# The low part of v's last 64 tokens moves from VectorE to GpSimd, the first exponentials wait for an early dummy one, and the order table is new

## The chip, the cores and the metric

The kernel runs on one core of one Trainium2 chip. Its time is the device time of an execution in microseconds (us). Three timed runs of the kernel before gave 339.54, 340.26 and 340.89 us; their median, 340.26 us, is the time that the changed kernel's is held against. A profile was taken in another execution, which took 337.29 us.

## The reference

Two blocks follow each other. The first is causal attention, for 4 batches and 12 heads, 448 tokens and a head size of 64, in float32:

```python
scores = scale * np.matmul(q, k.transpose(0, 1, 3, 2))
scores = np.where(mask, -1000000000.0, scores)
scores = scores - np.max(scores, axis=-1, keepdims=True)
attn = np.exp(scores)
attn = attn / (np.sum(attn, axis=-1, keepdims=True) + 1e-09)
return np.matmul(attn, v)
```

Its output, with the heads side by side, is the x (4 x 448 x 768) of a gated MLP, in which tokens are mixed through w_sg (448 x 448):

```python
h = x @ w_in                                  # 768 -> 1024, then the tanh form of gelu
u, v = (h[..., :d_ff // 2], h[..., d_ff // 2:])
v_n = (v - mu) / np.sqrt(var + 1e-06) * g_ln  # mean and variance over the 512 columns
v_s = np.einsum('ts,bsd->btd', w_sg, v_n) + b_sg[None, :, None]
return (x + (u * v_s) @ w_out)
```

## The kernel before

**Attention.** Two heads are one pair; there are 24 pairs, six to a batch. `pair(p)` loads q and k of a pair (`qk`), multiplies them on TensorE in two groups (`score(0)` and `score(1)`, line 431, tile `s` in PSUM), adds the mask and takes the negated row maxima on VectorE (line 446, `ngm`), and takes the exponentials on ScalarE (line 454), which sum their rows into `sm` and write the tile `P`. VectorE inverts the sums (lines 464 to 466), and two DMAs spread the result over the partitions (`rd`, then `rb`). For pairs 0 to 7 (below `FLIP`) TensorE transposes `P` (line 496, tiles `tx` and `ty`) and ScalarE or VectorE copies the result to `B` (lines 503 and 501). For the others VectorE transposes 32 x 32 blocks (line 484) and DMAs place them. TensorE then multiplies `B` by v (line 522, tile `o`), VectorE scales the result by `rb` into `xt` (line 549), and `keep_x` splits it into a rounded high part and the rest (lines 555 to 560, tile `x`). `P` has three buffers of two heads each, named P_90, P_91 and P_92 in the program's order; pair 2 of batch 0 uses P_92, pair 3 uses P_90 again.

**Weights.** All matrix multiplications of the MLP take float32 as a high part and a low part, three products for one. `split_w64` makes these parts of `w_in` and `w_out`: one operation on ScalarE (line 366), two on VectorE (368 and 370) and two on GpSimd (373 and 374), for each of 12 pieces of `w_in` (tile `vn`) and 16 of `w_out` (tile `g`).

**MLP of a batch.** `mlp(b)` has four parts: v for 128 tokens at a time and a last one of 64 tokens (`m` = 64), u, the mixing by `wsg` (tile `m<-wsg,vn`) and the output product (`m<-g,wout`); all multiplications are issued at line 577. v is normalised: statistics on VectorE, the power on GpSimd (line 621), the scaling on ScalarE (line 626). Then ScalarE copies it into a rounded high part, and the rest is subtracted: for the blocks of 128 tokens by GpSimd (line 631), for the last 64 tokens by VectorE (line 636). The tile `vn3` of these 64 tokens has the high part in partitions 0 to 63 and the low part in partitions 64 to 127, so that one multiplication takes both. Every mixing group ends with two multiplications by `vn3`.

**The order.** Nothing is issued while the functions run. `Order.add` records each operation with its engine and what it depends on, and gives it the next number. `run` then issues all operations in the order of the table `ORDER`, a list of these numbers written out by hand. `plan` only asserts that what an operation depends on stands ahead of it. Each engine works off its own operations in that order, and the framework adds the semaphores; SyncE issues all DMAs. The durations, sizes and `port` flags that `add` is given are read by nothing that runs. Seven small multiplications on a zeroed tile (`warm`, numbers 4 and 5 to 11, line 339) and one exponential of a constant column (number 3, line 330) do no work for the result.

Of the kernel before, what the change touches and what calls it, by code (L numbers as in the profile page):

```python
# [12 lines left out]
AF = mybir.ActivationFunctionType  # L13
ALU = mybir.AluOpType
# [211 lines left out]
def attention_gated_mlp(ctx: ExitStack, tc: tile.TileContext, qk, vP, w_in, g_ln, w_sgT, b_sg, w_out, out):  # L226
    nc = tc.nc
# [4 lines left out]
    DH = DF // 2  # L232
# [533 lines left out]
```

## Time and profile before

| what | value |
|---|---|
| median of three timed runs | 340.26 us (339.54 to 340.89) |
| the profiled execution | 337.29 us, of which the span of the instructions 335.5 us |
| TensorE (PE), matmuls | 324.1 us busy, 97% of the span, 2590 records |
| VectorE (DVE) | 251.0 us, 75% |
| ScalarE (ACT) | 208.5 us, 62% |
| GpSimd (POOL) | 175.9 us, 52% |
| chain that ended last | PE 93%, ACT 4%, DMA 1%, DVE 1% |
| mean granted TensorE clock | 0.994 of full speed |

The span begins with the first instruction and ends with the last. The profiled execution has 1.79 us outside it. "Busy" is the time in which at least one instruction of the engine ran. The share is over the whole span, so it says little of a single stage: ScalarE's 62% is a mean over a stage in which it never rests and one in which it mostly waits. The chain that ended last is followed back from the last instruction, at each step to what released it or to the instruction before it on its engine. In the rows below, PEld is TensorE's loading of weights, which overlaps its multiplications.

### The profile page before, as it was taken

What the parts mean: (1) busy time and instruction counts of PE and PEld (TensorE: products, weight loads), DVE (VectorE), ACT (ScalarE), POOL (GpSimd) and SP (SyncE); (2) the same over time, 40 slices, a digit from 0 to 9 for tenths busy, and PEclk for the clock granted to TensorE, in tenths of its full rate; (3) what the DMA queues carried; (4) which work ended last, traced back from release to release, by engine and by line L of the source; (5) the groups of instructions that cost most, each with busy time, mean ns of one, the idle gap of its engine ahead of it and who ended that gap; (6) DMA issues with size and microseconds to landing.
All of it is one profiled execution on the core that took longest, in us unless ns stands there. A gap on an engine that the chain in (4) does not pass through costs nothing.

```text
span 335.5 us, 7568 instructions
## 1 busy us (share of the span) xinstructions
PE 324.1 (97%) x2590; PEld 266.3 (79%) x2591; DVE 251.0 (75%) x762; ACT 208.5 (62%) x674; POOL 175.9 (52%) x225
## 2 busy tenths in 40 slices
PE   5699999999999999999999999999999999999995
PEld 3467678768887987878888978878989987889994
DVE  4899898999999888967977597889788531644613
ACT  1999999999894637666784526486674302355210
POOL 4258766888986964020535942014256824132691
PEclk9899999999999999999999999999999999999999
DMA  7889968595583688638747858739437440010004
GB/s 227 312 247 307 277 218 267 177 288 160 130 265 103 178 215 235 197 98 226 217 127 214 229 150 204 195 95 243 101 104 206 91 159 3 0 55 2 18 36 164
DMA packets 30965, 56.55 MB, mean 169 GB/s; under 512 B 6096, under 2 KB 15056, under 8 KB 30928
## 3 DMA queue, kind: packets, MB, share of 16 engines
q1 hardware_dynamic: 30928, 56.08, 57.5%
q8 instruction: 20, 0.33, 0.4%
q14 instruction: 17, 0.14, 0.1%
HBM read 33.39 MB, written 5.90 MB: 117 GB/s over the span
## 4 chain that ended last, share of the span: by engine, by line
PE 93%; ACT 4%; DMA 1%; DVE 1%; issue 0%; ACTq 0%; DVEq 0%
PE m L577 65%; PE o L522 13%; PE s L431 11%; ACT P L454 3%; PE ty L496 2%; PE tx L496 2%; DMA qk<-in_qk_dram 1%; PE m L339 0%; ACT L454 0%; ACT vn L366 0%; ACT B L503 0%; DVE s L446 0%; DVE res L702 0%; DVE ngm L446 0%; ACTq L454 0%
## 5 line engine op out<-in xcount | busy, mean ns | idle before, releaser
L454 ACT ACTIVATE P<-s,ngm 128x320 f32<-128x320 f32 (+3 forms) x240 | 102.7, 460 | 28.1 <-DVE ngm L446 19.7
L446 DVE CUSTOM_DVE_ANT_0 s<-s,mask 64x64 f32<-64x64 f32 (+3 forms) x192 | 77.6, 435 | 7.5 <-PE s L431 5.8
L577 PE MATMUL m<-win,x 128*128 128x512 f32 (+1 forms) x264 | 65.9, 399 | 0.0
L577 PE MATMUL m<-g,wout 128*128 128x448 f32 x288 | 61.1, 367 | 0.0
L577 PE MATMUL m<-x,win 128*128 128x448 f32 x288 | 61.1, 367 | 0.0
L577 PEld LDWEIGHTS m<-x,win 128*128 128x128 f32 x288 | 53.9, 188 | 5.0
L577 PEld LDWEIGHTS m<-g,wout 128*128 128x128 f32 x288 | 53.9, 188 | 5.0
L577 PEld LDWEIGHTS m<-win,x 128*128 128x128 f32 (+1 forms) x264 | 47.4, 183 | 11.7
L454 ACT ACTIVATION_READ_ACCUMULATOR P<-s,ngm 128x1 f32 (+1 forms) x240 | 55.1, 233 | 0.0
L431 PE MATMUL s<-qk 64*64 64x64 f32 (+5 forms) x768 | 45.2, 371 | 5.0 <-DMA qk<-in_qk_dram 4.4
L431 PEld LDWEIGHTS s<-qk 64*64 64x64 f32 x768 | 30.7, 139 | 21.6 <-issue 8.5
L522 PE MATMUL o<-B,vraw 128*64 128x64 f32 (+4 forms) x672 | 45.0, 291 | 0.0
L522 PEld LDWEIGHTS o<-B,vraw 128*64 128x64 f32 x672 | 32.8, 137 | 12.7 <-issue 4.5
L484 DVE STREAM_TRANSPOSE P<-P 128x1024 f32<-128x1024 f32 x32 | 38.2, 1224 | 0.7 <-DMA B<-P 0.6
L577 PE MATMUL m<-wsg,vn 128*128 128x448 f32 x176 | 38.3, 369 | 0.0
L621 POOL TENSOR_TENSOR mv<-mv,mhalf 128x1 f32<-128x1 f32 (+1 forms) x16 | 10.0, 626 | 49.0 <-DVE mv L619 40.7
L577 PEld LDWEIGHTS m<-wsg,vn 128*128 128x128 f32 x176 | 32.6, 188 | 3.6 <-DVE vn L636 0.4
L558 POOL TENSOR_TENSOR x<-xt,x 128x448 fp32r<-128x448 f32 x24 | 27.5, 1148 | 14.5 <-ACT x L557 14.2
L702 DVE TENSOR_TENSOR res<-m,res 128x448 f32<-128x448 f32 (+1 forms) x25 | 14.8, 603 | 23.2 <-PE m L577 15.2
L586 DVE SCALAR_TENSOR_TENSOR tmp<-tmp,m 128x448 f32<-128x448 f32 (+1 forms) x28 | 17.9, 640 | 16.2 <-ACT tmp L585 16.0
L673 POOL TENSOR_TENSOR tmp<-tmp,g 128x448 f32<-128x448 f32 x16 | 18.3, 1152 | 18.8 <-DVE tmp L669 18.8
L585 ACT ACTIVATE tmp<-m 128x448 f32<-128x448 f32 (+1 forms) x28 | 15.5, 562 | 20.3 <-PE m L577 19.2
(76 smaller groups left out, 410.8 us busy)
## 6 DMA issues: line engine op xcount, KB each, us to landing
B<-P SPq DMA_DIRECT2D x64, 256.0 KB
qk<-in_qk_dram SPq DMA_DIRECT2D x24, 448.0 KB
vn<-in_w_in_dram SPq DMA_DIRECT2D x12, 512.0 KB
vraw<-in_vP_dram SPq DMA_DIRECT2D x24, 256.0 KB
rb<-rd SPq DMA_DIRECT2D x24, 224.0 KB
out_dram<-res SPq DMA_DIRECT2D x9, 448.0 KB
g<-in_w_out_dram SPq DMA_DIRECT2D x16, 192.0 KB
out_dram<-res SPq DMA_DIRECT2D x5, 224.0 KB
```

Source lines behind the costliest of these rows:

```text
L431: nc.tensor.matmul(out=s[z][bk].t[64 * h:64 * h + 64, col:col + n], lhsT=qk_.t[r, 0, q0:q0 + 64], rhs=qk_.t[r, 1, k0:k0 + n], start=True, ...
L446: nc.vector.tensor_tensor_reduce(out=o, in0=i, in1=mk, scale=-0.125, scalar=3e38, op0=ALU.add, op1=ALU.min, accum_out=ngm[ib[z]][c][0:m])
L454: act(n, lambda c=c, m=m, k0=k0, n=n, bk=bk, col=col, off=off, kc=kc, i=i, z=z: nc.scalar.activation(out=P[i][0:m, off:off + n], in_=s[z][ ...
L484: dve(PW, lambda z=z: nc.vector.transpose(A[ia][:, :, :, z, :].rearrange("p g t k -> p t g k"), P[ib[z]]), Pk[z] + [kp], Ak, 1.105)
L496: nc.tensor.transpose(out, P[ib[z]][:, col:col + 128], ident)
L522: nc.tensor.matmul(out=dst(o.t[r]), lhsT=vr.t[:, c, r], rhs=src(z), start=first and n == 0, stop=last and n == len(lst) - 1)
L558: pool_tt(S, lambda: nc.gpsimd.tensor_tensor(out=y.t[:, S + 64:], in0=x.t, in1=f(y.t)[:, 0:S], op=ALU.subtract), [x, y], [(y, 1)])
L577: nc.tensor.matmul(out=ps.t[0:l().shape[1], 0:n], lhsT=l(), rhs=rr(), start=(k == 0), stop=(k == len(mms) - 1))
L585: act(n, lambda: nc.scalar.activation(out=z(), in_=h(), func=AF.Square), [ps], [t])
L586: dve(n, lambda: nc.vector.scalar_tensor_tensor(out=z(), in0=z(), scalar=1.0 / GC, in1=h(), op0=ALU.add, op1=ALU.mult), [ps], [t])
L673: pool_tt(S, lambda z=z, u=u: nc.gpsimd.tensor_tensor(out=z(), in0=z(), in1=u.t, op=ALU.mult), [u], [t])
L702: dve(hi - lo, lambda rr=rr, ps=ps, z=z, lo=lo, hi=hi: nc.vector.tensor_tensor(out=rr.t[:, z, lo:hi], in0=ps.t[:, lo:hi], in1=rr.t[:, z, l ...
```

## The change

- The low part of v's last 64 tokens is no longer one subtraction on VectorE, from partitions 0 to 63 into 64 to 127. ScalarE writes two more copies, the rounded one and the exact one, into partitions 64 to 127, and GpSimd subtracts there.
- Every exponential of the attention names "table", which the dummy exponential (number 3) writes, as something it depends on.
- `ORDER` is a new table. It has 1891 numbers, not 1883 (one VectorE operation less, two ScalarE and one GpSimd operations more in each of four batches), so the numbers behind the first such place are shifted.
- Some durations, sizes and `port` flags in `add` differ. `run` reads none of them.

```diff
 ORDER = (
-    84, 85, 86, 1, 4, 0, 2, 89, 87, 90, 96, 88, 95, 98, 91, 92, 97, 99, 93, 94, 125, 126, 128, 127, 12, 18, 13, 103,
+    0, 4, 1, 3, 2, 84, 125, 5, 6, 7, 8, 9, 166, 85, 86, 89, 87, 90, 96, 88, 95, 98, 97, 91, 93, 92, 99, 94, 100, 103,
...
-                    [s[z][bk], ("ngm", i, c), kp, ks] + ([("P", i, k - 1)] if k == 1 else [("P", i, 2)] if k == 4 else []),
+                    [s[z][bk], ("ngm", i, c), kp, ks, "table"] + ([("P", i, k - 1)] if k == 1 else [("P", i, 2)] if k == 4 else []),
...
                 y = buf(one, "vn3", [128, DH], F32R)
                 act(DH, lambda y=y, z=z: nc.scalar.activation(out=y.t[0:64], in_=z(), func=AF.Copy), [t], [y], True)
-                dve(DH, lambda y=y, z=z: nc.vector.tensor_tensor(out=y.t[64:128], in0=z(), in1=f(y.t)[0:64],
-                                                                 op=ALU.subtract), [t, y], [(y, 1)])
+                act(DH, lambda y=y, z=z: nc.scalar.activation(out=y.t[64:128], in_=z(), func=AF.Copy), [t], [(y, 1)], True)
+                act(DH, lambda t=t, z=z: nc.scalar.activation(out=t.t[64:128], in_=z(), func=AF.Copy), [], [t], True)
+                pool_tt(DH, lambda y=y, t=t: nc.gpsimd.tensor_tensor(out=y.t[64:128], in0=t.t[64:128],
+                                                                     in1=f(y.t)[64:128], op=ALU.subtract), [t], [(y, 1)])
```

Three lines are added in all, so a line behind line 64 of the kernel has a number higher by 1, and behind line 636 by 3.

**How the order moves, ScalarE in the first pairs.** Before, these rows stand ahead of the last exponential of pair 2 (tile P_92). L366 is the first step of a split of `w_in`; P_90 here is pair 3.

```order
L503 ACTIVATE B<-tx 128x512
L454 ACTIVATE P_92,sm_119<-s,ngm_111 128x320
L366 ACTIVATE vn<-vn 128x512
L454 ACTIVATE P_92,sm_119<-s,ngm_114 128x128
L454 ACTIVATE P_92,sm_119<-s,ngm_110 128x128
L366 ACTIVATE vn<-vn 128x512
L454 ACTIVATE P_92,sm_119<-s,ngm_115 128x320
L454 ACTIVATE P_92,sm_119<-s,ngm_112 128x448
L454 ACTIVATE P_92,sm_119<-s,ngm_110 64x64
L454 ACTIVATE P_92,sm_119<-s,ngm_109 64x64
L454 ACTIVATE P_90,sm_117<-s,ngm_96 128x448
L454 ACTIVATE P_92,sm_119<-s,ngm_114 64x64
```

In the changed kernel these rows stand ahead of the same place.

```order
L504 ACTIVATE B<-tx 128x512
L455 ACTIVATE P_92,sm_119<-s,ngm_116 128x448
L504 ACTIVATE B<-tx 128x512
L455 ACTIVATE P_92,sm_119<-s,ngm_113 64x64
L455 ACTIVATE P_92,sm_119<-s,ngm_112 128x448
L455 ACTIVATE P_92,sm_119<-s,ngm_111 128x320
L455 ACTIVATE P_92,sm_119<-s,ngm_109 64x64
L455 ACTIVATE P_92,sm_119<-s,ngm_110 128x128
L455 ACTIVATE P_92,sm_119<-s,ngm_110 64x64
L455 ACTIVATE P_92,sm_119<-s,ngm_115 128x320
L455 ACTIVATE P_92,sm_119<-s,ngm_114 128x128
L455 ACTIVATE P_92,sm_119<-s,ngm_114 64x64
```

From the start to this place ScalarE has five of the splits' operations and one exponential of pair 3 before, and three and none in the changed kernel; the 30 exponentials of pairs 0 to 2 and the six copies to `B` are the same. Up to the last exponential of pair 3 it is five splits and seven copies to `B` before, three and six in the changed kernel. The load of the exponential's table and the dummy exponential are ScalarE's first two instructions in the changed kernel; before, the load stands directly ahead of the first exponential of pair 0.

On SyncE, the loads of q and k of pairs 0, 1 and 2 are the first three in the changed kernel; before, pair 2's is the sixth, behind two pieces of `w_in` and one of v. Ahead of the first small DMA of the sums (`rd`) stand 13 loads in the changed kernel and 12 before.

**TensorE ahead of the first transposes of pair 2.** Before, these rows stand there; `o` is the product by v of pairs 0 and 1, `ty` the transposes, and the `s` rows are the first group of scores of pair 4.

```order
L522 MATMUL o<-B,vraw 64x448 x2
L522 MATMUL o<-B,vraw 64x320 x2
L522 MATMUL o<-B,vraw 64x64 x2
L522 MATMUL o<-B,vraw 64x128 x2
L522 MATMUL o<-B,vraw 64x64 x4
L496 MATMUL ty<-ident,P_92 128x128 x8
L431 MATMUL s<-qk 64x448 x2
L431 MATMUL s<-qk 64x384 x2
L431 MATMUL s<-qk 64x64 x2
```

In the changed kernel:

```order
L432 MATMUL s<-qk 64x448 x2
L432 MATMUL s<-qk 64x384 x2
L432 MATMUL s<-qk 64x64 x2
L523 MATMUL o<-B,vraw 64x64 x2
L523 MATMUL o<-B,vraw 64x128 x2
L523 MATMUL o<-B,vraw 64x64 x2
L523 MATMUL o<-B,vraw 64x448 x2
L523 MATMUL o<-B,vraw 64x320 x2
L523 MATMUL o<-B,vraw 64x64 x2
L523 MATMUL o<-B,vraw 64x128 x2
L523 MATMUL o<-B,vraw 64x64 x2
L497 MATMUL ty<-ident,P_92 128x128 x8
```

The first group of scores of pair 4 has moved from behind these transposes to ahead of them. Everything else that stands ahead of them is the same in both: the scores of pairs 0 to 3, the transposes and products by v of pairs 0 and 1, and the seven multiplications on zeros. Of these seven all stand ahead of pair 3's scores before; in the changed kernel five are TensorE's first work and two stand behind the first transposes of pair 0.

**The last 64 tokens of batch 1.** Before, VectorE subtracts (`vn_2449` is the `vn3` of batch 1) between operations of u:

```order
L466 STREAM_TRANSPOSE rT_122<-rs 128x32
L590 SCALAR_TENSOR_TENSOR g<-tmp,m 128x448
L484 STREAM_TRANSPOSE P_92<-P_90 128x8x4x32 x2
L586 SCALAR_TENSOR_TENSOR tmp<-tmp,m 128x448
L636 TENSOR_TENSOR vn_2449<-tmp,vn_2449 64x512
L586 SCALAR_TENSOR_TENSOR tmp<-tmp,m 128x448
```

In the changed kernel GpSimd does (`vn_2383` is the same tile); `x<-xt,x` are the low parts of a later pair's x, `res` the sums for batch 0's output.

```order
L561 TENSOR_TENSOR x<-xt,x 128x64
L692 TENSOR_TENSOR res<-x 128x448
L559 TENSOR_TENSOR x<-xt,x 128x448
L692 TENSOR_TENSOR res<-x 128x448
L639 TENSOR_TENSOR vn_2383<-tmp,vn_2383 64x512
L559 TENSOR_TENSOR x<-xt,x 128x448
```

The subtraction has moved to another engine's queue, behind a low part of x. On TensorE, the number of MLP multiplications between the end of v's last 64 tokens and the first mixing multiplication by `vn3` goes from 88 to 100 in batch 0, 88 to 79 in batch 1, 82 to 85 in batch 2, and stays 70 in batch 3.

## Rows read from the trace of the kernel before

**Rows 1.** Stages, TensorE: start:end, length, busy (records), granted clock, DMA share, GB/s.

```profile
8.83:22.65 13.82, 9.97 (x74) 0.88 0.81 279
22.65:60.00 37.35, 37.35 (x403) 1.00 0.86 268
140.00:331.87 191.87, 191.83 (x1375) 1.00 0.47 129
331.87:335.50 3.63, 0.00 (x0) 0.93 0.27 101
```

**Rows 2.** Stages, ScalarE, columns as above; the clock is still TensorE's.

```profile
7.07:31.09 24.02, 24.00 (x94) 0.93 0.86 286
31.09:50.00 18.91, 18.91 (x72) 1.00 0.83 258
84.00:100.00 16.00, 13.62 (x43) 1.00 0.72 203
```

**Rows 3.** The chain that ended last: start us, us, what.

```profile
3.92 1.88 PE s L431 x8
...
21.40 1.24 PE m L339 x5
...
28.04 1.02 PE ty L496 x8
29.07 0.92 PE s L431 x8
...
252.80 19.90 PE m L577 x96
```

**Rows 4.** Timeline, ScalarE: start us, us, operation; in brackets the idle time before.

```profile
7.07 1.28 ACT L454 ACT_TABLE_LOAD   x1 [7.07 <-DVE ngm L446]
8.37 0.63 ACT L454 ACTIVATE P<-s,ngm 128x448 f32<-128x448 f32 x1
...
23.70 0.81 ACT L366 ACTIVATE vn<-vn 128x512 f32<-128x512 f32 x1
24.26 0.65 ACT L454 ACTIVATE P<-s,ngm 128x320 f32<-128x320 f32 x1
...
29.41 0.75 ACT L503 ACTIVATE B<-ty 128x512 f32<-128x512 f32 x1
29.88 0.53 ACT L454 ACTIVATE P<-s,ngm 128x128 f32<-128x128 f32 x1
...
30.52 0.48 ACT L454 ACTIVATE P<-s,ngm 64x64 f32<-64x64 f32 x1
```

**Rows 5.** Two stretches, TensorE, columns as in rows 1.

```profile
7.30:14.12 6.82, 3.73 (x48) 1.00 1.02 389
14.13:17.53 3.40, 3.17 (x26) 0.50 0.46 132
```

**Rows 6.** Line 636: durations ns min/median/max; then who waited for it.

```profile
L636 DVE TENSOR_TENSOR vn<-tmp,vn x4: 685/685/2120, 97.8 to 308.4; 64x512 fp32r<-64x512 f32 x4
...
PEld m L577: 0.4, 2
```

**Rows 7.** Timeline: VectorE and TensorE in batch 1, GpSimd and VectorE in batch 2.

```profile
173.67 0.69 DVE L636 TENSOR_TENSOR vn<-tmp,vn 64x512 fp32r<-64x512 f32 x1
...
174.75 4.64 PE L577 MATMUL m<-wsg,vn 128*128 128x448 f32 x22
...
242.66 3.38 POOL L689 TENSOR_TENSOR res<-x 128x448 f32<-128x448 f32 x3
...
244.48 2.12 DVE L636 TENSOR_TENSOR vn<-tmp,vn 64x512 fp32r<-64x512 f32 x1 [1.02 <-ACT vn L635]
```

**Rows 8.** Groups by line: count, then busy us, mean ns, idle before us.

```profile
L631 POOL TENSOR_TENSOR vn<-tmp,vn 128x512 fp32r<-128x512 f32 x12 | 15.9, 1331 | 18.5 <-ACT vn L630 18.4
...
L635 ACT ACTIVATE vn<-tmp 64x512 fp32r<-64x512 f32 x4 | 2.5, 630 | 0.1
```

**Rows 9.** Waits: who for whom, us in total, times, longest us.

```profile
POOL x L558 <- ACT x L557: 14.2, 3, 6.6
```

More of the change, by code (lines that the diff above doesn't have):

```diff
@@ L328, in attention_gated_mlp @@
     od.add("pool", 2.4, consts3, w=["P", "sm", ("wsg", "pad")])
-    od.add("act", 0.2, lambda: nc.scalar.activation(out=pad[:, 0:1], in_=mhalf, func=AF.Exp), ["sm0"], ["table"])
+    od.add("act", 1.35, lambda: nc.scalar.activation(out=pad[:, 0:1], in_=mhalf, func=AF.Exp), ["sm0"], ["table"])
     def warm():
@@ L467, in inv @@
                                 rs.unsqueeze(2).broadcast_to([128, 2, 4, 4]))
-        od.add("dve", 0.42, inv, sk + [ks], [("rT", ip)])
+        od.add("dve", 0.573, inv, sk + [ks], [("rT", ip)])
         rb = buf(some[SLOTS["rb"]], "rb", [128, S])
@@ L474, in pair @@
         dma(lambda: nc.sync.dma_start(out=rb.t, in_=bass.AP(
-            tensor=rd[ip].tensor, offset=rd[ip].offset, ap=[[512, 8], [0, 16], [1, S]])), [("rd", ip)], [rb], 320e3, dur=0.56)
+            tensor=rd[ip].tensor, offset=rd[ip].offset, ap=[[512, 8], [0, 16], [1, S]])), [("rd", ip)], [rb], 360e3, dur=0.56)
         Pk = [[("P", i, c) for c in range(5)] for i in ib]
@@ L579, in group, with gelu2 @@
             pe(per * len(mms[a:a + cut]), go, rd, [ps])
-    def gelu2(ps, m, n, dst=None):
+    def gelu2(ps, m, n, dst=None, port=False):
         t = buf(three, "tmp", [128, 512])
@@ L586, in gelu2 @@
         dve(n, lambda: nc.vector.scalar_tensor_tensor(out=z(), in0=z(), scalar=1.0 / GC, in1=h(), op0=ALU.add,
-                                                      op1=ALU.mult), [ps], [t])
+                                                      op1=ALU.mult), [ps], [t], port=port)
         act(n, lambda: nc.scalar.activation(out=z(), in_=z(), func=AF.Tanh, scale=GS * GC), [], [t], True)
@@ L590, in gelu2 @@
         dve(n, lambda: nc.vector.scalar_tensor_tensor(out=z() if dst is None else d.t, in0=z(), scalar=1.0, in1=h(),
-                                                      op0=ALU.add, op1=ALU.mult), [ps, t], [d])
+                                                      op0=ALU.add, op1=ALU.mult), [ps, t], [d], port=port)
         return t, z
@@ L614, in mlp @@
                                                                      op=ALU.add), [ps], [hs])
-                t, z = gelu2(hs, m, DH)
+                t, z = gelu2(hs, m, DH, port=True)
             st, mv = buf(two, "st", [128, 6]), buf(two, "mv", [128, 3])
@@ L622, in mlp @@
                 out=mv.t[0:m, 1:2], in0=mv.t[0:m, 1:2], in1=mhalf[0:m], op=ALU.pow), ["sm0"], [mv])
-            od.add("dve", 0.07, lambda mv=mv, m=m: nc.vector.tensor_scalar(
+            od.add("dve", 0.125, lambda mv=mv, m=m: nc.vector.tensor_scalar(
                 out=mv.t[0:m, 2:3], in0=mv.t[0:m, 0:1], scalar1=mv.t[0:m, 1:2], scalar2=-1.0, op0=ALU.mult, op1=ALU.mult),
@@ L626, in mlp @@
             act(DH, lambda mv=mv, z=z, m=m: nc.scalar.activation(
-                out=z(), in_=z(), func=AF.Identity, scale=mv.t[0:m, 1:2], bias=mv.t[0:m, 2:3]), [mv], [t], True)
+                out=z(), in_=z(), func=AF.Identity, scale=mv.t[0:m, 1:2], bias=mv.t[0:m, 2:3]), [mv], [t], True, 2)
             if m == 128:
```

179 rows, old and new, of the table ORDER are left out of this document.

## The prediction

> **What bounds the kernel now.** I read the stages of TensorE first. From 22.65 us on it is busy for 37.35 of 37.35 us, then up to 331.87 us for 191.83 of 191.87 us in the last long stretch [rows 1]. The last 3.63 us hold no multiplication. The change leaves TensorE's useful work as it is, so the end can move by two things only: how much of this work is done before TensorE saturates at 22.65 us, and new waits behind it. In the stretch before, TensorE is busy for 9.97 of 13.82 us [rows 1], and part of that does nothing for the result: five of the seven multiplications on zeros take 1.24 us of the chain [rows 3], and the clock is at 0.50 (1.2 of 2.4 GHz) for 3.40 us [rows 5].
>
> Next I ask what TensorE waits for in that head. ScalarE starts at 7.07 us with the load of a table [rows 4] and is busy for 24.00 of 24.02 us and then for 18.91 of 18.91 us, to 50 us [rows 2]. So ScalarE, which gives the exponentials, is the tight engine of the head, and TensorE's lead can hardly grow by more than ScalarE's.
>
> **The change, part by part.**
>
> *Table load.* Before, ScalarE loads the table after VectorE's first maxima, at 7.07 us, and the first exponential begins at 8.37 us [rows 4]: 1.30 us on ScalarE's path. Now load and dummy exponential stand first in its queue, where it idles for 7.07 us. The dummy waits for one small VectorE operation behind the zeroing of the multiplications' tile, all of it ahead of the first load of q and k, so this cover is wide. Gain: 1.30 us.
>
> The Trainium skill (ScalarE: Activation LUTs, What ACT_TABLE_LOAD costs) adds a drain to each switch and comes to about 2.66 us in all; by that rule the term would be 1.36 us larger and the sum with it. The trace does not agree: the exponential begins 0.02 us behind the load [rows 4].
>
> *ScalarE's new order.* Up to the last exponential of pair 3 (30.52 us), two splits of w_in and one copy to B have gone from ahead of it to behind it. A split takes 24.26 - 23.70 = 0.56 us from start to start, a copy 29.88 - 29.41 = 0.47 us [rows 4]: 2 x 0.56 + 0.47 = 1.59 us. This work is not gone, and ScalarE stays full to 50 us [rows 2], so it comes due there; the two VectorE and two GpSimd operations of each split move along with it. Bounds: 0 (all is paid back by new waits of TensorE) to 1.59 us (TensorE is never late for it). Between them I take half, 0.8 us, since both rows hold at once: ScalarE has no rest up to 50 us, and TensorE from 22.65 us on has no wait.
>
> *The first scores and the clock.* The first group of scores took 1.88 us; a later one, of the same size, takes 0.92 us [rows 3]. TensorE had done nothing before it. Five multiplications on zeros now run there. They could have the first group run at the full clock, and VectorE's maxima start up to 0.96 us earlier. Against that stands the stretch from 7.30 to 14.12 us, in which TensorE was busy for 3.73 of 6.82 us and after which the clock fell to 0.50 [rows 5]: work with pauses did not keep the full clock there, and the five are followed by a pause until the first load lands. Bounds: 0.96 us gained, or, if a second stretch at half clock comes, 3.17 / 2 = 1.6 us lost [rows 5]. I take 0.3 us, nearer to nothing.
>
> The Trainium skill (TensorE: Matmul & The Clock Gate, Part 1) says that a monitor of TensorE's recent activity sets the clock, and that one kernel's start differs from run to run. By that rule this term would be 0.96 us in some executions and nothing in others, and the sum 2.9 or 1.9 us. That the granted clock fell after a half-idle stretch [rows 5] agrees; no run here shows the difference between executions.
>
> *TensorE's own order.* Its first transposes of pair 2 begin at 28.04 us [rows 3]. To begin them 2.4 us earlier (the three terms above) it has to have done the first group of pair 4's scores too, 0.92 us [rows 3], but the zeros no longer stand there, over 1.24 us. What is left, some 2.1 us, fits into the 13.82 - 9.97 = 3.85 us that it idles between 8.83 and 22.65 us [rows 1]. Cost: 0; without that cover up to 0.92 us, which is work done early, not lost.
>
> *Low part of the last 64 tokens.* VectorE loses four subtractions, three of about 0.69 us and one of 2.12 us [rows 6, 7]; it is not the bound there. ScalarE gains two copies a batch of 0.63 us, GpSimd one subtraction; I take the 1.33 us of 128 rows [rows 8]. ScalarE idles there, 16.00 - 13.62 us in the fullest of these stretches [rows 2]. Path to the first multiplication by vn3: + 2 x 0.63 + 1.33 - 0.69 = + 1.90 us in batches 0, 1 and 3, and + 0.47 us in batch 2. What covers it is the multiplications between, at 19.90 / 96 = 0.207 us each [rows 3]: 12 more in batch 0 (2.48 us), 9 fewer in batch 1 (1.86 us), 3 more in batch 2 (0.62 us), as many in batch 3. So batches 0 and 2 come out ahead and can win back what TensorE waited for line 636, 0.4 us in two waits [rows 6]. Batch 1 needs 1.90 + 1.86 = 3.76 us; it has from 174.36 us (end of the subtraction) to 174.75 + 15 x 0.207 = 177.86 us, where the first vn3 stands behind 15 mixing multiplications [rows 7]: 3.5 us, so 0.3 us are lost. Batch 3 loses between 0 and 1.90 us; TensorE did not wait there, so I take 0.3 us. Sum: 0.4 - 0.3 - 0.3 = - 0.2 us; ends + 0.4 and - 2.2 us.
>
> The Trainium skill (SBUF — State Buffer, Who interferes with whom) says that a VectorE instruction with two inputs in SBUF and a GpSimd instruction that reads SBUF block each other entirely. The subtraction that took 2.12 us beside GpSimd's sums, against 0.69 us [rows 6, 7], agrees. By that rule the new GpSimd subtraction can be held too, by VectorE's steps on the same 64 tokens alone; batch 3 would then cost its full 1.90 us, and the sum 0.6 us instead of 2.2 us.
>
> *Loads.* SyncE issues the third pair's q and k ahead of the weights now, and 13 loads ahead of the first small DMA of the sums, not 12. Cost: 0, as TensorE's only wait for a load that the chain holds is the first one, which ends at 3.92 us [rows 3] and is still issued first. The 16 DMA engines are busy for 0.81 and 0.86 of these stretches [rows 1], so a late one is possible: 0.3 us to either side.
>
> *Sum.* 1.30 + 0.8 + 0.3 - 0.2 = 2.2 us. The profiled execution took 337.29 us: 335.50 us of span and 1.79 us around it; it would take 335.1 us. The three timed runs have a median of 340.26 us, 2.97 us above it, with the same program; I take the gain from that: 338.1 us.
>
> **The rivals.**
>
> *Paid back.* The deferred splits and copies reach TensorE as new waits between 25 and 50 us, and VectorE's maxima hold the exponentials there as well. Then at most the table load is left, and half of it more likely than all: 340.26 - 0.65 = 339.6 us. For it: ScalarE has no rest to 50 us [rows 2]. Against it: no wait of TensorE in that stretch [rows 1], so the exponentials were early enough even with the later start.
>
> *GpSimd's queue, slower.* In batch 1 the subtraction stands behind a low part of x, which waits for ScalarE's copy of x. Three such waits took 14.2 us, the longest 6.6 us [rows 9]. If it meets one like the longest, vn3 is late by all of it, since the slack of batch 1 is spent: 338.1 + 6.6 = 344.7 us. It decides from a wait of 2.2 + 1.7 = 3.9 us on. For it: the place in the queue, and 9 multiplications less of cover. Against it: 21 of the 24 had no wait of weight.
>
> *The table load stalls for longer than its row.* ScalarE's path would lose more than 1.30 us: 336.7 us with the drain of the page named above. Against it: nothing stands between 7.07 and 8.37 us but the load.
>
> **How the numbers follow.** My forecast, a gain of 1.3 to 3.4 us (336.9 to 339.0 us), has 0.58; paid back 0.28; GpSimd's queue 0.09; the longer stall 0.05. A measurement of this kernel tells about 0.5% from no change, here 1.7 us. Of the forecast's 0.58 about 0.06 lies below that, so faster has 0.52 + 0.05 = 0.57, the same 0.06 + 0.28 = 0.34, slower 0.09. The range goes from 336.2 us (the largest terms, 1.30 + 1.59 + 0.96 + 0.4 = 4.25 us, nearly reached) to 340.4 us (all paid back, and a little lost in the v part).
>
> **What would show it.** The table load ahead of everything on ScalarE, and the first exponential some 1.3 us earlier, at about 7.1 us or before. The last exponential of pair 3 at about 28 us instead of 30.52 us. TensorE's saturation beginning about 2 us earlier in work done, at most a few waits of 0.2 to 0.8 us up to 50 us, and a span of about 333.3 us. The clock's fall to 0.50 earlier, later or gone. No wait of TensorE for GpSimd at the mixing multiplications. The forecast is wrong if the waits between 25 and 60 us add up to 2 us or more, if TensorE waits for line 639 by more than 0.5 us in a batch, or if the first exponential is not earlier.

## The result, and the profile after

The changed kernel takes 344.66 us (median of four runs, 343.97 to 345.63), the kernel before 339.9 us beside it: a ratio of 1.0147, 95% interval 1.0099 to 1.0196. A gain of 2.2 us was forecast; 4.8 us were lost, and the time lies outside the predicted range. The profiled execution took 344.71 us (span 342.9 us), that of before 337.29 us.

The head went as forecast. ScalarE's timeline, columns as in [rows 4]:

```profile
0.73 1.28 ACT L331 ACT_TABLE_LOAD   x1 [0.73 <-PEq L758]
...
7.05 0.63 ACT L455 ACTIVATE P<-s,ngm 128x448 f32<-128x448 f32 x1 [4.76 <-DVE ngm L447]
...
27.55 0.50 ACT L455 ACTIVATE P<-s,ngm 128x128 f32<-128x128 f32 x1
...
28.50 0.84 ACT L367 ACTIVATE vn<-vn 128x512 f32<-128x512 f32 x1
```

The first exponential begins at 7.05 us and not at 8.37, pair 3's last one at 27.55 us and not at 30.52 [rows 4], and a split of w_in now stands behind it. Then the lead goes. TensorE by stretches, columns as in [rows 1], the last one a piece of the first:

```profile
22.65:112.00 89.35, 82.18 (x717) 0.98 0.64 199
22.65:60.00 37.35, 34.34 (x377) 1.00 0.70 221
72.43:75.84 3.41, 3.41 (x16) 0.50 0.30 113
```

Before, TensorE had no rest from 22.65 us on [rows 1]. Now it idles for 89.35 - 82.18 = 7.17 us up to 112 us, and for 3.41 us its clock is at 0.50 (1.2 of 2.4 GHz), which costs 3.41 / 2 = 1.7 us. From 112 us on it is full again. What it waited for: who, for whom, us in total, times, longest us:

```profile
PE s L432 <- DVE tmp L591: 2.7, 1, 2.7
PE o L523 <- DVE B L502: 2.4, 2, 2.2
...
PE m L578 <- DVE g L591: 0.7, 1, 0.7
```

All three are VectorE, and none is line 639, the new subtraction. The waits end at 49.15, 70.89 and 104.82 us. So I looked at VectorE's groups by line and shape: count, busy us, mean ns, idle us before. Before, the two steps of a weight split (lines 368 and 370):

```profile
L370 DVE SCALAR_TENSOR_TENSOR vn<-vn 128x512 int32<-128x512 int32 x12 | 8.3, 690 | 0.6 <-ACT vn L366 0.5
L370 DVE SCALAR_TENSOR_TENSOR g<-g 128x192 int32<-128x192 int32 x16 | 6.2, 405 | 0.0
L368 DVE TENSOR_SCALAR vn<-vn 128x512 int32<-128x512 int32 x12 | 5.1, 425 | 0.1
L368 DVE TENSOR_SCALAR g<-g 128x192 int32<-128x192 int32 x16 | 5.0, 333 | 0.0
```

After, the same steps, one line further down:

```profile
L371 DVE SCALAR_TENSOR_TENSOR vn<-vn 128x512 int32<-128x512 int32 x12 | 11.4, 954 | 0.0
L371 DVE SCALAR_TENSOR_TENSOR g<-g 128x192 int32<-128x192 int32 x16 | 9.6, 612 | 0.0
L369 DVE TENSOR_SCALAR vn<-vn 128x512 int32<-128x512 int32 x12 | 8.0, 674 | 0.0
L369 DVE TENSOR_SCALAR g<-g 128x192 int32<-128x192 int32 x16 | 8.0, 521 | 0.0
```

As many steps, as many elements, and 37.0 us where it was 24.6: 12.4 us more. The summary of line 371 (minimum, median, maximum in ns) says that not all steps grew, but some by a lot:

```profile
L371 DVE SCALAR_TENSOR_TENSOR g<-g x16: 332/358/1457, 53.3 to 108.0; 128x192 int32<-128x192 int32 x16
L371 DVE SCALAR_TENSOR_TENSOR vn<-vn x12: 660/692/1647, 14.8 to 91.2; 128x512 int32<-128x512 int32 x12
```

Which ones, the timeline tells. VectorE in front of two of the waits:

```profile
46.43 0.80 DVE L369 TENSOR_SCALAR vn<-vn 128x512 int32<-128x512 int32 x1
47.15 1.34 DVE L369 TENSOR_SCALAR g<-g 128x192 int32<-128x192 int32 x1
48.41 0.68 DVE L502 COPY B<-ty 128x512 f32<-128x512 f32 x1
...
62.81 1.46 DVE L371 SCALAR_TENSOR_TENSOR g<-g 128x192 int32<-128x192 int32 x1
64.19 1.64 DVE L371 SCALAR_TENSOR_TENSOR vn<-vn 128x512 int32<-128x512 int32 x1
```

GpSimd at the same time:

```profile
46.28 0.66 POOL L374 CAST win<-vn 128x512 fp32r<-128x512 f32 x1
47.02 1.36 POOL L375 TENSOR_TENSOR win<-vn,win 128x512 fp32r<-128x512 f32 x1
48.34 0.61 POOL L561 TENSOR_TENSOR x<-xt,x 128x64 fp32r<-128x64 f32 x2
...
62.69 1.36 POOL L375 TENSOR_TENSOR win<-vn,win 128x512 fp32r<-128x512 f32 x1
64.02 1.26 POOL L354 TENSOR_TENSOR wsg<-tmp,wsg 128x448 fp32r<-128x448 f32 x1
```

Of the 56 steps 25 are over 0.1 us longer than the median of their kind in the kernel before. All of them begin while an operation of GpSimd runs, and 24 end 0.1 to 0.6 us behind its end: the one of 62.81 us at 64.27, GpSimd's at 64.05. I call such a step held. Nine more steps begin beside GpSimd and do not grow like that. The copy of 48.41 us reads PSUM and keeps its 0.68 us beside GpSimd's operation of 48.34 us, but it comes late, and TensorE waits for it until 49.15 us. The Trainium skill (SBUF — State Buffer, Who interferes with whom) says that a VectorE instruction with two inputs in SBUF and a GpSimd instruction that reads SBUF contend, that a VectorE instruction in a mode that uses both ports contends with GpSimd too, the later one waiting for the whole of the earlier one, and that a VectorE instruction with at most one SBUF input outside these modes does not. These rows agree: the long steps of line 371 have two inputs in SBUF, the copy has none. Those of line 369 have one; that they are in such a mode these rows do not show.

### The profile page after: what moved, and what is told of

It reads as the page before. It is cut to its first block, busy times and chain, and to the rows that moved or that the text cites. A ratio compares the mean times of both kernels' runs of the same rounds, so it can differ in the third digit from the quotient of the medians.

```text
span 342.9 us, 7565 instructions
## 1 busy us (share of the span) xinstructions
PE 329.0 (96%) x2591; PEld 267.1 (78%) x2591; DVE 257.3 (75%) x758; ACT 212.5 (62%) x682; POOL 180.0 (53%) x229
## 4 chain that ended last, share of the span: by engine, by line
PE 71%; ACT 10%; DVE 9%; DMA 4%; issue 3%; POOL 2%; DVEq 0%; ACTq 0%
PE m L578 53%; PE o L523 10%; PE s L432 7%; ACT P L455 6%; DVE s L447 3%; DMA rb<-rd 2%; PE tx L497 1%; DVE g L371 1%; DMA qk<-in_qk_dram 1%; DVE g L369 1%; DMA rd<-rT 1%; DVE vn L371 1%; POOL x L559 1%; DVE vn L369 1%; ACT g L367 1%
## 5 line engine op out<-in xcount | busy, mean ns | idle before, releaser
L455 ACT ACTIVATE P<-s,ngm 64x64 f32<-64x64 f32 (+3 forms) x240 | 101.0, 444 | 37.5 <-DVE ngm L447 31.1
L578 PE MATMUL m<-win,x 128*128 128x512 f32 (+1 forms) x264 | 67.0, 401 | 0.0
L455 ACT ACTIVATION_READ_ACCUMULATOR P<-s,ngm 128x1 f32 (+1 forms) x240 | 52.0, 218 | 0.0
L432 PE MATMUL s<-qk 64*64 64x64 f32 (+5 forms) x768 | 47.8, 369 | 4.1 <-DVE tmp L591 2.7
L559 POOL TENSOR_TENSOR x<-xt,x 128x448 fp32r<-128x448 f32 x24 | 28.2, 1182 | 9.9 <-ACT x L558 9.6
L692 POOL TENSOR_TENSOR res<-x 128x448 f32<-128x448 f32 x24 | 27.3, 1150 | 7.3 <-DMA out_dram<-res 7.2
L622 POOL TENSOR_TENSOR mv<-mv,mhalf 128x1 f32<-128x1 f32 (+1 forms) x16 | 9.1, 566 | 40.3 <-DVE mv L620 40.3
L632 POOL TENSOR_TENSOR vn<-tmp,vn 128x512 fp32r<-128x512 f32 x12 | 15.6, 1297 | 23.7 <-ACT vn L631 21.1
```

The costliest lines, as they stand in the source:

```text
L432: nc.tensor.matmul(out=s[z][bk].t[64 * h:64 * h + 64, col:col + n], lhsT=qk_.t[r, 0, q0:q0 + 64], rhs=qk_.t[r, 1, k0:k0 + n], start=True, ...
L455: act(n, lambda c=c, m=m, k0=k0, n=n, bk=bk, col=col, off=off, kc=kc, i=i, z=z: nc.scalar.activation(out=P[i][0:m, off:off + n], in_=s[z][ ...
L559: pool_tt(S, lambda: nc.gpsimd.tensor_tensor(out=y.t[:, S + 64:], in0=x.t, in1=f(y.t)[:, 0:S], op=ALU.subtract), [x, y], [(y, 1)])
L578: nc.tensor.matmul(out=ps.t[0:l().shape[1], 0:n], lhsT=l(), rhs=rr(), start=(k == 0), stop=(k == len(mms) - 1))
L622: od.add("pool", 0.46, lambda mv=mv, m=m: nc.gpsimd.tensor_tensor(out=mv.t[0:m, 1:2], in0=mv.t[0:m, 1:2], in1=mhalf[0:m], op=ALU.pow), ["s ...
L632: pool_tt(DH, lambda y=y, z=z: nc.gpsimd.tensor_tensor(out=y.t[:, 1, :], in0=z(), in1=f(y.t)[:, 0, :], op=ALU.subtract), [t, y], [(y, 1)])
```

## The experiments

Each ratio is to the kernel before, timed beside it, with its 95% interval. In some kernels the written-out order takes a few lines more or less, so line 371 may be 372 to 378 there.

**low_undone.** New order, VectorE's subtraction again:

```diff
-                act(... out=y.t[64:128], in_=z() ...)
-                act(... out=t.t[64:128], in_=z() ...)
-                pool_tt(DH, ... out=y.t[64:128], in0=t.t[64:128], in1=f(y.t)[64:128] ...)
+                dve(DH, ... out=y.t[64:128], in0=z(), in1=f(y.t)[0:64] ...)
```

> The changed kernel with its new order table, but the low part of v's last 64 tokens is subtracted by VectorE again (at the place in the order where GpSimd's subtraction stood; the two copies by ScalarE are gone). Theory H (VectorE held): the new order sets VectorE's two steps of each weight split, lines 369 and 371, beside running operations of GpSimd, and their sum grows from 24.6 to 37.0 us; VectorE is late at 49.15, 70.89 and 104.82 us, whatever computes the low part. It expects 343 to 345.5 us, and gaps of 2 us or more at about 49 and 71 us. Rival L (low part): GpSimd's queue behind its new subtraction makes the kernel slower; it expects 338 to 340 us here. Rival D (loads): the new order of the loads makes rb land late (7.62 us after its issue); it too expects 343 to 345.5 us.

Measured: 346.96 us, 1.0233 (1.0200 to 1.0266). The two waits of 2.7 and 2.2 us stand where they stood, so the new low part is not their cause. The kernel is even slower, and slower than H gave, by a wait of 1.9 us for VectorE's own subtraction, at whose end (109.19 us) the clock falls to 0.50 for another 3.41 us. Rival L falls.

**low_alone.** The other half alone: old order, the diff above the other way round, the three steps at the old one's place.

> The kernel before with its old order, and the low part of v's last 64 tokens as in the changed kernel (two more copies by ScalarE and GpSimd's subtraction stand where VectorE's subtraction stood); nothing else of the change. Theory H and rival D: the low part is nearly free, 339 to 341 us, and the prediction's term for it (-0.2 us, bounds +0.4 and -2.2) holds. Rival L: 342 to 345 us.

Measured: 346.35 us, 1.0222 (1.0194 to 1.0250). Missed: in the old order the low part costs 7 us. ScalarE's timeline in batch 0:

```profile
99.18 0.63 ACT L639 ACTIVATE vn<-tmp 64x512 fp32r<-64x512 f32 x1
99.72 1.03 ACT L592 ACTIVATE tmp<-tmp 128x448 f32<-128x448 f32 x2
100.65 0.51 ACT L458 ACTIVATE P<-s,ngm 128x320 f32<-128x320 f32 x1
...
101.70 0.63 ACT L640 ACTIVATE vn<-tmp 64x512 fp32r<-64x512 f32 x1
102.23 0.61 ACT L641 ACTIVATE tmp<-tmp 64x512 f32<-64x512 f32 x1
```

and TensorE's:

```profile
104.30 3.67 PE L581 MATMUL m<-wsg,vn 128*128 128x448 f32 x10 [3.40 <-POOL vn L642]
```

The second copy stands behind two tanh steps and two exponentials; TensorE waits 3.40 us, and its clock is at 0.50 from 103.9 to 107.3 us.

**not_held.** New order, all of the change; the two steps replaced by ones that kept their time beside GpSimd:

```diff
-        dve(n, lambda: nc.vector.tensor_scalar(out=lo(), in0=lo(), scalar1=29, ... logical_shift_right), ...)
-        dve(n, lambda: nc.vector.scalar_tensor_tensor(out=lo(), in0=hi(), scalar=3, in1=lo(), ...), ...)
+        dve(n, lambda: nc.vector.transpose(lo(), lo()), ...)
+        dve(n, lambda: nc.vector.transpose(lo(), hi()), ...)
```

> The changed kernel with its new order, in which the two VectorE steps of each split of w_in and w_out (lines 369 and 371) are transposes of the same tile, with 512 or 192 elements a partition as before; the weights are then not the right ones, all else is computed as before. The transposes of line 485 took 1.23 us for 1024 elements beside GpSimd's work and alike without it, so these should take about 0.62 and 0.26 us and not grow beside GpSimd. Theory H: VectorE's time in these steps falls from 37.0 us to some 25 us, the gaps at about 49 and 71 us shrink to under 0.5 us together, the clock does not fall at 72 us, and the kernel takes 336 to 339 us. Rivals D and L: the gaps stay, 342 to 345 us.

Measured: 334.66 us, 0.987 (0.985 to 0.989): below the forecast. VectorE's groups, then TensorE's stretch:

```profile
L373 DVE STREAM_TRANSPOSE vn<-vn 128x512 int32<-128x512 int32 x12 | 8.2, 688 | 0.0
L372 DVE STREAM_TRANSPOSE vn<-vn 128x512 int32<-128x512 int32 x12 | 8.2, 688 | 0.0
L373 DVE STREAM_TRANSPOSE g<-g 128x192 int32<-128x192 int32 x16 | 5.5, 355 | 0.0
L372 DVE STREAM_TRANSPOSE g<-g 128x192 int32<-128x192 int32 x16 | 5.3, 354 | 0.0
```

```profile
22.65:112.00 89.35, 89.16 (x806) 1.00 0.73 223
```

The steps take 27.2 us, more than the right ones in the kernel before (24.6 us), and yet 10.0 us come back (9.4 us by the two ratios): 7.17 - 0.19 = 7.0 us of waits and the 1.7 us of the clock; 1.3 us I can't place. TensorE's order is the same in both kernels, so they can be held against each other multiplication by multiplication: the changed kernel is late by 2.5 us at 49.15 us, by 5.5 us at 70.89 us, by 7.6 us at 75.59 us and by 10.2 us both at 114.24 us and at the end. Rival D falls with it, since the loads are issued in the same order.

**head_then_before.** The change with its order up to the 184th number, then the old order:

```diff
-ORDER = new[0:1891]
+ORDER = new[0:184] + [n for n in old if n not in new[0:184]]
```

> All of the change, but its new order only for the first 184 of 1891 numbers (to pair 4's scores, about 22 us: the table first, five multiplications on zeros first, the new order of the first 17 loads); from there on what is left stands in the old order. Theory H: the lead of 1.5 us that the changed kernel has at 22.65 us is kept, since the old order held only 4 of VectorE's 56 steps; 337.5 to 339.5 us. Rival D: rb and the loads ahead of it are late as in the changed kernel, 342 to 345 us. Rival L: 341.5 us or more.

Measured: 347.87 us, 1.0263 (1.0239 to 1.0288). All missed. TensorE waits 4.6 us for line 642, as in low_alone, and 2.9 us at 41.59 us before it multiplies by w_in; the chain holds a load of w_in there. The kernel mixes three causes, and tells nothing between H and D.

**before_not_held.** The control: the diff of not_held in the kernel before.

> The kernel before, unchanged in order, with the same replacement as in the run that took 334.66 us: the two VectorE steps of each weight split are transposes, so the weights are not the right ones. Theory H (the new order sets these steps beside running operations of GpSimd, the old one does not): the old order has little to gain, since only 4 of its 56 steps were longer than alone; 337.5 to 340 us. Rival S (transposes suit any order, and the 10 us came from something else in them): about as much as in the new order, 329 to 335 us.

Measured: 338.79 us, 0.9998 (0.9983 to 1.0013). H is right: the old order has nothing to gain there.

**table_alone.** The first term of the sum by itself:

```diff
-    84, 85, 86, 1, 4, 0, 2, 89, ...
+    84, 85, 86, 1, 3, 4, 0, 2, 89, ...
-                    [s[z][bk], ("ngm", i, c), kp, ks] + ...
+                    [s[z][bk], ("ngm", i, c), kp, ks, "table"] + ...
```

> The kernel before with one edit: the table is loaded first in ScalarE's queue, and the exponentials depend on it. All else, the order of all other steps too, is as before. The prediction's first term (1.30 us off ScalarE's path) and theory H with few steps held: 337 to 338.5 us, the first exponential at about 7.1 us. Rival F (the old order is fitted to its times, so that any shift of ScalarE sets VectorE's steps beside GpSimd's or brings new waits): 340.5 us or more, with more than 27 us in lines 368 and 370 or a gap of TensorE behind 22 us.

Measured: 337.42 us, 0.9955 (0.9939 to 0.9971), or 1.65 us less; the first exponential begins at 7.16 us. It is the fastest kernel here that computes everything, faster than both.

**bank15.** A changed kernel that still computes the weights, with an operand of each step in PSUM:

```diff
+        h = bank("h") if key in BANK else None
+        low = lambda: h.t.bitcast(I32)[:, 0:n] if h else lo()
-        ... tensor_scalar(out=lo(), in0=lo(), scalar1=29, ...)
-        ... scalar_tensor_tensor(out=lo(), in0=hi(), scalar=3, in1=lo(), ...)
+        ... tensor_scalar(out=low(), in0=lo(), scalar1=29, ...)
+        ... scalar_tensor_tensor(out=lo(), in0=hi(), scalar=3, in1=low(), ...)
```

> The changed kernel, all of it computed as it should be, its order unchanged; in 15 of the 28 weight splits (10 of w_in, 5 of w_out) VectorE's first step writes to a PSUM bank and its second step reads that bank, so that neither has all its operands in SBUF. VectorE's steps with an operand in PSUM (lines 587 and 591, 0.60 to 0.68 us) did not grow beside GpSimd. Theory H: the 30 steps take some 0.7 and 0.4 us beside GpSimd too, the gap at 71 us shrinks to under 0.7 us, the clock does not fall there, and the kernel takes 336 to 341 us; the 13 other splits are still held. Rival P (the hold does not ask where the operands are): 343.5 to 346 us.

Measured: 356.97 us, 1.0533 (1.0512 to 1.0554). Half right: the operands' place is what H says, the time is far off. VectorE's groups up to 120 us:

```profile
L376 DVE TENSOR_SCALAR h<-vn 128x512 int32<-128x512 int32 x9 | 6.2, 705 | 0.8 <-ACT B L511 0.8
L378 DVE SCALAR_TENSOR_TENSOR vn<-vn,h 128x512 int32<-128x512 int32 x9 | 6.0, 679 | 1.3 <-ACT vn L372 1.3
...
L378 DVE SCALAR_TENSOR_TENSOR g<-g 128x192 int32<-128x192 int32 x10 | 5.1, 508 | 0.0
```

With an operand in PSUM the second step is not held (679 ns against 954). The first one is not held either, but takes 705 ns, where its mean was 674 ns in the changed kernel and 425 ns in the kernel before, so it wins nothing. The second steps on 192 elements that are left in SBUF are still held (508 ns). TensorE idles for 15.7 us between 20 and 120 us, in most places for exponentials or VectorE, and its clock is at 0.50 in three stretches of 3.41 us. I take it that the kernel's eight PSUM buffers, which scores, transposes and products share, have become the bound; no run tests that. So no kernel here that computes the right weights in the new order wins the 10 us back.

**low_close.** As low_alone, but the two copies and the subtraction stand right behind the first copy:

```diff
-    ..., 510, 522, 532, 840, 844, 511, 512, 513, ...
+    ..., 510, 511, 512, 513, 522, 532, 840, 844, ...
```

> The kernel before with the new low part, as in the run that took 346.35 us, but ScalarE's two more copies and GpSimd's subtraction stand right behind the first copy of v's last 64 tokens in the order, in all four batches; there the second copy stood behind two steps and two exponentials and began at 101.70 us, 1.9 us after the first had ended, and TensorE waited 3.40 us at 104.30 us, behind which the clock fell. Theory Q (the place in ScalarE's queue): the subtraction ends 1.9 us earlier, the gap is 1.3 to 1.7 us, the clock does not fall, and the kernel takes 341.5 to 343.5 us. Rival E (the edit as such: its three more steps one behind the other): 345 us or more.

Measured: 342.18 us, 1.0098 (1.0070 to 1.0125), and a wait of 1.53 us up to 101.56 us, behind which the clock does not fall. Theory Q: 4.2 of the 7 us were the place in ScalarE's queue.

**two_late.** The second term by itself, in the old order:

```diff
-ORDER: 31 to 35 and 37 to 41 (two splits of w_in) at 105 to 158, 48 (a load) at 141
+ORDER: 31 to 35 at 150 to 200, 48 at 206, 37 to 41 at 239 to 286
```

> The kernel before with one edit to its order: the splits of the fourth and fifth chunk of w_in's second half (ten steps of ScalarE, VectorE and GpSimd) stand about where the new order has them, behind pair 3's last exponentials, and one later load waits for their tile. All else is as before. This is the prediction's second term by itself. The prediction: two splits of 0.56 us leave ScalarE's path, half of it is kept, 338 to 339 us, and at worst all is paid back, 339.1 us. Theory H: VectorE's moved steps meet running operations of GpSimd, or the moved load comes late; over 340.5 us, with more than 26 us in lines 368 and 370 or a gap of TensorE behind 30 us.

Measured: 346.65 us, 1.0239 (1.0204 to 1.0275). Slow as H has it, but by its second cause: VectorE waits 2.28 and 1.73 us, up to 47.06 and 49.42 us, for rb, which stands on SyncE behind the moved load, and TensorE's clock is at 0.50 from 49.0 us for 6.8 us.

**warm_early** and **table_warm.** The third term, alone and with the first:

```diff
+ORDER: 4, 5, 6, 7, 8, 9 (zeroing and five multiplications) first; 10, 11 behind pair 0's transposes
```

> The kernel before with the multiplications on zeros placed as the change has them: the zeroing of their tile first on VectorE, five first on TensorE, the other two behind pair 0's transposes; the table load and all else as before. The prediction's third term by itself: 0.3 us gained (bounds 0.96 gained, 1.6 lost), 338.8 us. Theory C (what counts is the clock: the changed kernel and three of its kin had no stretch at half clock in the head, the kernel before one of 3.4 us at 14.1 us): the stretch at half clock is gone, and up to 3.4 / 2 = 1.7 us with it; 337.3 to 338.5 us. Rival F (the old order is fitted to its times): 339.5 us or more.

> The kernel before with both: the table first, as in the run that took 337.42 us, and the multiplications on zeros placed as the change has them; all else as before. If the prediction's first and third term add up: 1.65 + 0.3 to 1.7 us less, 335.7 to 337.1 us, which would be faster than both kernels. Rival F: the second shift costs what it gives, 337.2 us or more.

Measured: 339.31 us, 1.0014 (0.9982 to 1.0047), and 337.66 us, 0.9982 (0.9956 to 1.0008). The five early multiplications give nothing that can be measured, and both edits together are not clear of no change. Theory C falls: the profile of warm_early has its stretch at half clock, from 14.5 to 17.9 us.

**low_undone_not_held.** The diffs of not_held and low_undone together.

> The changed kernel with its new order, transposes in place of VectorE's steps of the weight splits (so the weights are not the right ones), and the low part of v's last 64 tokens subtracted by VectorE again. Against the run with transposes and the new low part (334.66 us) it measures the prediction's fifth term in the new order without the held steps. The prediction (the low part costs 0.2 us, between 0.4 gained and 2.2 lost): 332.5 to 335.1 us, 334.5 likeliest. Rival G (the low part by GpSimd is worth 2 us in the new order, as with the held steps: 346.96 against 344.66 us): 336 to 337.5 us.

Measured: 335.16 us against 334.66 us (ratios 0.9897, 0.9862 to 0.9933, and 0.987). Without held steps the new low part is worth about 0.5 us in the new order, less than the two intervals tell apart.

**two_late_2, two_late_2_not_held** and **w_in_not_held.** two_late with the load 48 behind both loads of rb; the same with transposes; the changed kernel with transposes in w_in's splits alone.

> The kernel before with the same ten steps of two splits of w_in moved back as in the run that took 346.65 us; there the load that waits for their tile stood ahead of the loads of rb on SyncE, rb was issued at 40.91 us, and VectorE and TensorE waited for it, so that run did not tell of the splits alone. Now this load stands behind the two loads of rb. The prediction's second term: 338 to 339.1 us. Theory H: the moved VectorE steps are held by GpSimd (line 373 took 1.65 us at 34.46 us, line 371 1.32 us at 43.46 us), 340 to 343 us. Rival Y (SyncE's queue alone made that run slow): 338 to 339.5 us with the steps held all the same.

> The same order, with transposes in place of VectorE's steps of all weight splits (the weights are not the right ones). Theory H: what the moved splits cost goes, 336.5 to 339 us, and 1 us or more less than with the right steps. Rival Y: no difference of over 0.7 us between the two.

> The changed kernel with its new order, with transposes in the 12 splits of w_in alone; the 16 splits of w_out are as they are (w_in is then not right). The w_in steps carry 6.1 of the 12.5 us by which VectorE's steps grew (19.5 us in the changed kernel, 13.4 us in the kernel before). Theory H with a share for each: half of the 10 us come back, 338 to 341 us, and the gap at 70.89 us, whose VectorE chain holds both kinds, is cut to about half.

Measured: 342.58 us, 1.0092 (1.0056 to 1.0128); 342.65 us, 1.0096 (1.0062 to 1.0130); 338.45 us, 0.9975 (0.9955 to 0.9996). In the old order the two moved splits cost 3.5 us, and not by the hold: without it the time is the same. Who TensorE waits for in two_late_2:

```profile
PE s L434 <- ACT P L457: 1.9, 2, 1.1
PE ty L499 <- ACT P L457: 1.1, 3, 0.5
PE tx L499 <- DVE B L504: 1.0, 1, 1.0
PE tx L499 <- ACT P L457: 0.7, 1, 0.7
```

These are many small waits, mostly for exponentials; which step starts them stays open. H has the time right and the mechanism wrong; Y has the missing difference right and the time wrong. In the changed kernel w_in's splits carry 344.66 - 338.45 = 6.2 of the 10.0 us, and the wait of 2.7 us falls to 1.2 us, as H has it.

## Why the prediction was wrong

*Table load, 1.30 us.* Right: the exponential is 1.32 us earlier, and alone the edit gives 1.65 us. No drain behind the load shows: in table_alone the dummy begins 0.02 us behind it, as [rows 4] had it.

*ScalarE's new order, 0.8 us of 0 to 1.59.* The step that failed. "This work is not gone" was right, and so was the sentence that two VectorE and two GpSimd operations of each split move along, but these were counted at nothing, and "all is paid back" was taken for the worst end. There is no such floor. The term also looked at two splits of w_in only, while the new order sets all of VectorE's and GpSimd's operations anew: the held steps begin between 28.25 and 108.04 us, in the splits of w_in and of w_out, and no term of the sum stands for them. By the timelines 25 of the 56 steps are over 0.1 us longer than the median of their kind before, where 6 were; the longest is held for 1.15 us (1.57 against 0.42), and 12.4 us come together. That took 10 us from a kernel that would have gained 4.5 us (334.66 against 339.13 us). The two splits by themselves, moved back in the old order, cost 3.5 us and gained none (two_late_2); that was not the hold, and its cause stays open.

The 4.5 us are twice the forecast 2.2 us. The table (1.65 us) and the low part (0.5 us) make up about half of them; no run says what the rest is, so the forecast of a gain is not borne out term by term either.

A number that would have warned of it was in the trace and not read. VectorE in the kernel before, columns as in [rows 2]:

```profile
22.65:60.00 37.35, 34.51 (x136) 1.00 0.86 268
60.00:112.00 52.00, 50.24 (x162) 1.00 0.64 188
```

It rests for 89.35 - 84.75 = 4.6 us while the weights are split, which 12.4 us more do not fit into. (A small rest alone is no harm: in not_held VectorE rests for 89.35 - 85.91 = 3.4 us there, and TensorE waits for 0.19 us.) I read ScalarE as full and TensorE as full, and did not ask for the third. Six of its 56 steps were long already, four of them by over 0.2 us, so the price of one was there too: at 58.20 us line 370 took 1.31 us for 192 elements, and 0.35 in most places. The rule of the Trainium skill (SBUF — State Buffer, Who interferes with whom) was weighed in the prediction for the subtractions of the low part only; the steps of the splits, with their operands in SBUF, were held as well.

*First scores and clock, 0.3 us.* The first group still takes 1.88 us. Not shown to give anything. Nor does the mean clock of a run show in its time: of the 23 runs of the kernel before that were timed beside warm_early, the four with a mean granted clock of 1.000 took 337.8 to 339.5 us, the eight at 0.990 or less 337.5 to 340.6 us.

*TensorE's own order, 0.* Right: in not_held only 0.19 us of waits are left from 22.65 to 112 us.

*Low part, - 0.2 us.* The serial path (+ 1.90 us) was sized rightly: from the end of the first copy to the end of the subtraction it is 2.73 us in batch 0, and 0.82 us before. But the cover depends on the order: 0.5 us are gained in the new one without held steps, 2.3 us with them (346.96 against 344.66 us), 3.1 to 7 us lost in the old. The gain of 2.3 us is beyond the upper bound of 0.4: in low_undone VectorE's own subtraction came late too, and the clock fell there once more.

*Loads, 0.* Not run alone. rb landed 7.62 us after its issue, and VectorE idled 0.84 us for it; not_held shows that this order of loads allows 334.66 us.

*The rivals.* "Paid back" named the right kind of wait, with a floor that does not exist. "GpSimd's queue" gives 344.7 us, which is the time measured, by a mechanism that did not happen: nobody waited for line 639. A number that fits is no proof.

## What to carry to other kernels

When an order moves work, price every engine's part of it, and ask each engine's rest in that stage, not only the fullest one's. Before VectorE steps like these two move, with all operands in SBUF, see what GpSimd does at the new place: one that begins just after a GpSimd operation has begun can wait for nearly all of it, as at 62.81 us. The transposes did not wait. An order that was fitted to its times is no neutral base: the low part alone, or two splits moved alone, cost it 3 to 8 us, so halves of a change need not add up.

## What the runs showed of the hardware

TensorE's clock fell to half for 3.41 us 1.5 us behind the wait of 2.69 us, and 0.4 us before the end of the one of 3.40 us in low_alone; it did not fall behind the one of 2.17 us. The length of a wait alone does not tell: in low_undone the clock fell at the end of a wait of 1.92 us (109.19 us), in bank15 it did not fall behind one of 3.34 us (65.17 us). In the head the clock differs for the same first 80 us of program; low_alone, then low_close, TensorE, columns as in [rows 1], against 3.40 us in [rows 5]:

```profile
11.61:18.44 6.83, 6.38 (x43) 0.51 0.63 218
```

```profile
13.55:20.39 6.84, 5.88 (x38) 0.53 0.63 206
```

The Trainium skill (TensorE: Matmul & The Clock Gate, Part 1) says that a kernel's start differs from run to run; the prediction could not show it, these rows do. VectorE's transposes of SBUF (688 ns for 512 elements) were not held in any of the 56 steps of not_held, 39 of which began while GpSimd ran.
